# One written order for four engines in the turns of a packed attention and soft-MoE kernel

## The chip, the cores and the metric

The kernel runs on one core of a Trainium2 chip. The metric is the device time of one execution in microseconds. TensorE is PE in the tables (PEld its weight loads), VectorE DVE, ScalarE ACT, GpSimd POOL, and SyncE SP, which here only issues DMAs.

## What is computed

Shapes: q, k and v are 8 batches x 8 heads x 576 x 64, p holds 32 queries per head, phi is 512 x 32, w1 is 8 x 512 x 1024, w2 is 8 x 1024 x 512, and all is float32.

```python
def sm_attn(qq, kk, vv):
    a = softmax(scale * qq @ kk.T)
    return a @ vv
p_packed = sm_attn(p, k, v)
x = sm_attn(q, p_packed, p_packed)        # then [4608, 512]: heads side by side
logits = x @ phi
slot_input = softmax(logits, over rows).T @ x
slot_out[e] = relu(slot_input[e] @ w1[e]) @ w2[e]
out = softmax(logits, over slots) @ slot_out
```

Each softmax subtracts its maximum and adds 1e-9 to its sum.

## The kernel before

The work goes in 8 turns. Turn i has four heads (g = i % 2) of two batches (dd = i // 2, a "double"), so a pair of turns makes one double. In the loop over turns 0 to 6 (from L757), turn i has three kinds of work at once:

- For turn i + 1 the first scores. `kp` (L213) transposes k in 18 pieces on PE, into PSUM banks of four (t0 = 0, 4, 8), and copies each bank to kT; `s1` (L228) makes the 8 score products, the negated maximum nm on DVE (L250), the Exp on ACT (L254, its result a1) and a small copy a1e on POOL.
- For turn i the packed heads and the second scores. `ap` (L265) and `at` (L280) transpose a1 and copy it to a1T and a1tail; `ppm` (L288) multiplies with v into the bank m; `ppn` divides by the sums (rz), giving ppd; `pt` (L321) transposes ppd in the same bank and copies it to ppT in two halves; `mp` multiplies with phi. `qp` (L351) transposes q in 18 pieces and copies to qT. `s2p`, `s2m` and `s2s` (L370, L394, L400) make the second scores s in three parts c = 0, 1, 2, their maxima mx and the subtraction into a2, and `e2` (L431) is one Exp over all of a2.
- For turn i - 1 the rest. `n2` sums a2 on DVE (z, L442), takes the reciprocal (L449) and multiplies a2 on POOL (L450). `a2p` (L453) transposes a2 in 9 pieces and copies them to a2T, and `lg` (L470) makes the logits lp, which go to LT.

Every second turn (3 and 5) also finishes a double: `f1` to `f4`, `gz`, `gr`, `gt`, `gs` (L502 to L712) update the running maximum, the sums z_run and the slot inputs S_run (tiles post, mx, rw, gr, rt, rb). Each second turn prepares a new p (`pre_p`, L188, tile tp).

What sets the order: each helper issues its PE products and behind them their copies. `evac` (L81) gives a copy to ACT or DVE by a running count of estimated load, if no engine is named. In the loop no order is fixed; a scheduler arranges each engine's instructions by priority (the order of the code) and by when it thinks them ready. Turn 7 and what ends the attention stand in `manual_schedule` (L870), where the order of the code is the order on PE, DVE, ACT and POOL. Engines run their queues in order. PSUM banks rotate: `pstr` has 4, for k, q, a1, a2, tp, mx and the second scores, `ps1` holds one first score, `psm` one m, `psp` one of lp, post or gr.

DMAs are issued by SP in the order of the code: per turn v, k and q of later turns (L99 to L141), then the weights (L734, L741). q, k, v and the weights share a ring of 15 tiles of 1 MB (L57), so a load waits for the tile that stood there 15 loads earlier; their small tails share 6. Behind the loop more pools open for weights when others are closed. Behind the attention come layer 1 (hp, L991), layer 2 (so, L1040, and for the last expert sb, L1134), and the output.

Of the kernel before, what the change touches and what calls it, by code (L numbers as in the profile page):

```python
# [23 lines left out]
def pack_attention_soft_moe(  # L24
# [162 lines left out]

    def pre_p(dd):  # L188
        pn = pns[dd]
        pnd = kpool.tile([P, NG, 2, 2, D], F32, tag="pnd", name=f"pnd_{dd}")  # L190
        pT = kpool.tile([P, NG, 8, NS // 2, 2], F32, tag="pT", bufs=2, name=f"pT_{dd}")
        for x in range(2):
            nc.vector.tensor_copy(pnd[:, :, :, x, :], pn.rearrange("p g (s d) -> p g s d", s=2))
        tp = bank(pstr, f"tp{dd}")
        for g in range(NG):
            for j in range(2):
                nc.tensor.transpose(
                    tp[:, (2 * g + j) * P : (2 * g + j + 1) * P],
                    pnd[:, g, j].rearrange("p x d -> p (x d)"),
                    ident,  # L200
                )
        for g in range(NG):
# [118 lines left out]
    def pt(i):  # L321
# [3 lines left out]
        for b2 in range(2):  # L325
            nc.tensor.transpose(
                tp[:, b2 * P : (b2 + 1) * P], s["ppd"][:, b2].rearrange("p x d -> p (x d)"), ident
            )
        tpv = tp.rearrange("p (b h s) -> p b h s", b=2, h=4)
        nc.vector.tensor_copy(ppT[0:D, :, :, 1, :], tpv[0:D])  # L330
        nc.vector.tensor_copy(ppT[D:P, :, :, 0, :], tpv[D:P])  # L331

    def mp(i):
# [4 lines left out]
        for b2 in range(2):  # L338
            for a in range(2):
# [6 lines left out]
                )  # L346
        mm = lpool.tile([P, 2, NSLOT], F32, tag="mm", bufs=2, name=f"mm_{i}")
        nc.scalar.copy(mm.rearrange("p b x -> p (b x)"), mq)
        s["mm"] = mm

    def qp(i, m0, eng=None):  # L351
# [4 lines left out]
        if m0 == 0:  # L356
            s["qT"] = tpool.tile([P, 2 * T, P], F32, tag="qT", name=f"qT_{i}")
# [6 lines left out]
        evac(s["qT"][:, m0 : m0 + nt].rearrange("p t x -> p (t x)"), tp[:, 0 : nt * P], eng)  # L364
# [27 lines left out]

    def s2m(i, c):
# [6 lines left out]
    def s2s(i, c):  # L400
# [3 lines left out]
            s["a2"][:, t0 : t0 + nt].rearrange("p t h s -> p h t s"),  # L404
# [11 lines left out]
    def e2d(i, c):  # L416
# [3 lines left out]
            s["a2"][:, t0 : t0 + nt].rearrange("p t h s -> p h t s"),  # L420
# [33 lines left out]
    def a2p(i, c, eng=None):  # L454
# [15 lines left out]
    def lg(i, pool=psp):  # L470


        dd, g = divmod(i, NG)
        s = st[i]
        lp = bank(pool, f"lp_{i}")
        for b2 in range(2):
# [9 lines left out]
        for c in range(4):  # L486
# [6 lines left out]
            )  # L493
        if g == 0:
# [7 lines left out]
    def f1(dd):  # L502
        f1a(dd)
        f1b(dd)

    def f1a(dd):
# [8 lines left out]
        nc.scalar.activation(dL, LT, AF.Exp, bias=nm, scale=1.0, accum_out=zg)  # L515
        nc.vector.tensor_scalar_mul(mt, nm, -1.0)
        x["mt"], x["zg"], x["dL"] = mt, zg, dL

    def f1b(dd, pool=psp):
        x = du[dd]  # L520
        LT, dL = x["LT"], x["dL"]
        d = qpool.tile([P, T, NSLOT], F32, tag="d", name=f"d_{dd}")
        df = d.rearrange("p t s -> p (t s)")
        Ls = L_sb[:, dd].rearrange("p t s -> p (t s)")
        x["d"] = d

        b = bank(pool, f"post_{dd}")
        for y, src in enumerate((LT, dL)):
            for j in range(2):
                o = y * W + j * P  # L530
                nc.tensor.transpose(b[:, o : o + P], src[:, j * P : (j + 1) * P], ident)
        nc.vector.transpose(df[:, W : W + 32], dL[:, W : W + 32])
        nc.scalar.copy(df[:, 0:W], b[:, W : 2 * W])
        nc.vector.transpose(Ls[:, W : W + 32], LT[:, W : W + 32])
        nc.scalar.copy(Ls[:, 0:W], b[:, 0:W])
# [687 lines left out]
```

## Time and profile before

| | us |
|---|---|
| median of 3 runs | 222.86 |
| lowest and highest | 220.75, 227.43 |
| the profiled execution | 222.83 |
| its span in the trace | 221.1 |

The span goes from the first instruction to the last on the core; 1.7 us of the execution lie around it. Durations come from that one execution. In a timeline, instructions of one group that follow closely are merged: the start, then the stretch they take together, then their number, and in brackets how long the engine stood idle ahead of them and what released it. A product of float32 is two PE instructions in the trace for some shapes. [...]

### The profile page before, as it was taken

What the parts mean: (1) busy time and instruction counts of PE and PEld (TensorE: products, weight loads), DVE (VectorE), ACT (ScalarE), POOL (GpSimd) and SP (SyncE); (2) the same over time, 40 slices, a digit from 0 to 9 for tenths busy, and PEclk for the clock granted to TensorE, in tenths of its full rate; (3) what the DMA queues carried; (4) which work ended last, traced back from release to release, by engine and by line L of the source; (5) the groups of instructions that cost most, each with busy time, mean ns of one, the idle gap of its engine ahead of it and who ended that gap; (6) DMA issues with size and microseconds to landing.
All of it is one profiled execution on the core that took longest, in us unless ns stands there. A gap on an engine that the chain in (4) does not pass through costs nothing.

```text
span 221.1 us, 6708 instructions
## 1 busy us (share of the span) xinstructions
PE 188.4 (85%) x2811; PEld 127.8 (58%) x2811; DVE 120.5 (54%) x279; ACT 116.3 (53%) x253; POOL 25.0 (11%) x40
## 2 busy tenths in 40 slices
PE   1787799998996999899999988998999999989700
PEld 1655576685783688578688757875633333456300
DVE  2221576259387237648955717897679170288800
ACT  2277466956753675675675694745322000188800
POOL 3000003004003000400300220043021000000000
PEclk9999999999999799999999999999999999999955
DMA  4999999999999999579999989999789999159996
GB/s 134 325 312 318 334 342 334 289 267 337 306 314 298 360 313 355 145 246 390 412 406 406 387 299 385 345 397 411 261 314 350 414 406 407 59 209 414 408 416 262
DMA packets 39198, 72.33 MB, mean 327 GB/s; under 512 B 11648, under 2 KB 23168, under 8 KB 39168
## 3 DMA queue, kind: packets, MB, share of 16 engines
q1 hardware_dynamic: 39168, 71.90, 93.2%
q8 instruction: 22, 0.36, 0.7%
q14 instruction: 8, 0.07, 0.1%
HBM read 62.46 MB, written 9.44 MB: 325 GB/s over the span
## 4 chain that ended last, share of the span: by engine, by line
PE 53%; ACT 17%; DVE 10%; DMA 7%; issue 4%; SPq 3%; ACTq 0%; DVEq 0%
PE s L387 8%; PE kp L223 6%; PE s L243 6%; DMA v<-in_v_dram 6%; PE so L1040 5%; ACT a L254 5%; PE m L297 3%; PE op L1165 3%; ACT kT L88 3%; PE gr L641 3%; PE hp L991 2%; ACT qT L88 2%; PE ap L272 2%; PE lp L479 2%; ACT a1T L88 2%
## 5 line engine op out<-in xcount | busy, mean ns | idle before, releaser
L88 ACT COPY kT<-kp 128x512 f32<-128x512 f32 (+1 forms) x42 | 19.1, 484 | 24.9 <-PE kp L223 24.9
L450 POOL TENSOR_TENSOR a<-a,z 128x1152 f32<-128x1152 f32 (+1 forms) x8 | 16.0, 1996 | 71.2 <-DVE z L449 58.7
L223 PE MATMUL kp<-ident,k 128*128 128x128 f32 x128 | 20.9, 307 | 2.2 <-DMA k<-in_k_dram 1.3
L254 ACT ACTIVATE a<-s,nm 128x576 f32<-128x576 f32 x16 | 21.6, 1352 | 1.6 <-DVE nm L250 1.6
L88 ACT COPY qT<-qp 128x512 f32<-128x512 f32 (+1 forms) x40 | 20.2, 558 | 3.5 <-PE qp L363 3.1
L387 PE MATMUL s<-ppT,qT 128*64 128x64 f32 x576 | 20.6, 225 | 1.1 <-DVE ppT L331 0.3
L387 PEld LDWEIGHTS s<-ppT,qT 128*64 128x64 f32 x576 | 18.3, 138 | 4.8 <-ACT qT L88 3.7
L250 DVE TENSOR_REDUCE nm<-s 128x1 f32<-128x576 f32 x16 | 11.9, 745 | 16.8 <-PE s L243 16.8
L223 PEld LDWEIGHTS kp<-ident,k 128*128 128x128 f32 x128 | 16.1, 157 | 7.4 <-ACT a1T L88 1.7
L243 PE MATMUL s<-kT,pT 64*32 64x288 f32 x256 | 16.8, 437 | 3.8 <-ACT kT L88 3.0
L397 DVE TENSOR_REDUCE mx<-s 128x16 f32<-128x512 f32 (+1 forms) x24 | 12.5, 551 | 11.5 <-PE s L387 11.5
L363 PE MATMUL qp<-ident,q 128*128 128x128 f32 x128 | 18.2, 278 | 0.0
L88 ACT COPY a1T<-ap 128x512 f32<-128x512 f32 x16 | 8.7, 589 | 17.1 <-PE ap L272 17.1
L363 PEld LDWEIGHTS qp<-ident,q 128*128 128x128 f32 x128 | 15.1, 145 | 1.9 <-issue 1.9
L991 PE MATMUL hp<-w,xz 128*32 128x512 f32 x128 | 14.4, 594 | 0.5 <-DVE xz L1092 0.5
L442 DVE TENSOR_REDUCE z<-a 128x36 f32<-128x1152 f32 (+2 forms) x9 | 10.9, 1207 | 6.4 <-ACT a L433 6.4
L1165 PE MATMUL op<-sh,cT 128*128 128x512 f32 x35 | 12.7, 455 | 0.8 <-DVE cT L91 0.3
L1040 PE MATMUL so<-w,hT 128*32 128x512 f32 x112 | 12.4, 592 | 0.0
L91 DVE COPY ob<-op 128x512 f32<-128x512 f32 x17 | 11.3, 689 | 1.3 <-PE op L1165 0.9
L459 PE MATMUL a2p<-ident,a 128*128 128x128 f32 x72 | 11.0, 280 | 0.5 <-ACT a L419 0.4
L88 ACT COPY a2T<-a2p 128x512 f32<-128x512 f32 (+1 forms) x24 | 11.1, 510 | 0.6 <-PE a2p L459 0.5
L297 PE MATMUL m<-v,a1T 128*32 128x64 f32 x512 | 9.7, 221 | 1.9 <-ACT a1T L88 1.4
(156 smaller groups left out, 302.3 us busy)
## 6 DMA issues: line engine op xcount, KB each, us to landing
w<-in_moe_w_dram SPq DMA_DIRECT2D x64, 512.0 KB, 8.0
out_dram<-ob SPq DMA_DIRECT2D x11, 768.0 KB, 5.8
k<-in_k_dram SPq DMA_DIRECT2D x16, 512.0 KB, 6.6
q<-in_q_dram SPq DMA_DIRECT2D x16, 512.0 KB, 6.9
v<-in_v_dram SPq DMA_DIRECT2D x16, 512.0 KB, 7.4
kx<-in_k_dram SPq DMA_DIRECT2D x16, 64.0 KB, 6.1
qx<-in_q_dram SPq DMA_DIRECT2D x16, 64.0 KB, 6.5
vx<-in_v_dram SPq DMA_DIRECT2D x16, 64.0 KB, 6.9
```

The lines of the kernel that those rows point to most:

```text
L88: nc.scalar.copy(dst, src)
L223: nc.tensor.transpose(tp[:, j * P : (j + 1) * P], src, ident)
L243: nc.tensor.matmul(ps[hs, x, 0:HALF], pTs[dd][xs, g, 4 * b2 + h].rearrange("p a s -> p (a s)"), kT[xs, :, hs], start=True, stop=True,)
L254: nc.scalar.activation(a1.rearrange("p (r t x) -> p x t r", t=T, x=2), ps[:, :, 0:HALF].rearrange("p x (t r) -> p x t r", t=T), AF.Exp, bi ...
L297: nc.tensor.matmul(s["m"][hs, b2 * D : (b2 + 1) * D], s["a1T"][:, 4 * b2 + j, hs] if j < 4 else a1tail[:, b2, hs], vm[:, b2, h, j * D : (j ...
L363: nc.tensor.transpose(tp[:, j * P : (j + 1) * P], qf[:, o : o + P], ident)
L387: nc.tensor.matmul(o, s["qT"][:, m, 64 * x : 64 * x + 64], w, start=True, stop=True)
L397: nc.vector.tensor_reduce(mx, s[f"s2{c}"], axis=AX.X, op=ALU.max)
L450: eng.tensor_tensor(a2, a2, z2.unsqueeze(3).broadcast_to([P, nt, 4, NS]), op=ALU.mult)
L991: nc.tensor.matmul(hp[nh][32 * a : 32 * a + 32, :], xzf[:, (4 * e + a) * NSLOT : (4 * e + a + 1) * NSLOT], w1s[e, a // 2][:, a % 2, nh * 5 ...
L1040: nc.tensor.matmul(so[32 * a : 32 * a + 32, :], hTf[:, (NJ * e + j) * NSLOT : (NJ * e + j + 1) * NSLOT], w2s[e, j // 4][:, j % 4, :], star ...
L1165: nc.tensor.matmul(op, cT[:, o, :], sh, start=True, stop=True)
```

## The change

The helpers are cut into parts, so that a group of PE products and the copies of its result can stand apart, and every copy's engine is named. A function `parts(i)` gives the parts of turn i by name, and one string, `PAIR`, names some 135 parts of two turns (those of the second with a ') in the order in which they are issued, `:a` or `:d` behind a copy saying ACT or DVE. The loop goes over pairs, inside `manual_schedule` for PE, DVE, ACT and POOL. The last pair has only turn 6. `START` does the same for the first scores and q of turn 0. The finish of a double stays in its second turn, with `f1` now there too. The stretch behind the loop keeps its order with the new names. The products, the copies and the loads stay the same in number and kind; SP's order does not change.

```diff
-    def kp(i, b2):
-        kT = kpool.tile([P, T, P], F32, tag="kT", bufs=2, name=f"kT_{i}_{b2}")
-        for t0, nt in ((0, 4), (4, 4), (8, 1)):
-            tp = bank(pstr, f"kp_{i}_{b2}_{t0}")
...
-            evac(kT[:, t0 : t0 + nt].rearrange("p t x -> p (t x)"), tp[:, 0 : nt * P])
+    def kt(i, b2, t0):
+        tp = bank(pstr, f"kp_{i}_{b2}_{t0}")
+        for t in range(t0, min(t0 + 4, T)):
+            src = main[:, b2, t * P : (t + 1) * P] if t < 8 else tail[:, b2]
+            nc.tensor.transpose(tp[:, (t - t0) * P : (t - t0 + 1) * P], src, ident)
+    def ke(i, b2, t0, eng):
...
+        evac(
+            s[f"kT{b2}"][:, t0 : t0 + nt].rearrange("p t x -> p (t x)"),
+            s[f"kp{b2}{t0}"][:, 0 : nt * P],
+            eng,
+        )
...
+    PAIR = """
+        load ap0 ape0:d ap1 k04 ke04:a k00 ke00:a q0 ape1:d k08 m0 z2 ke08:a rz s10 q8 z2r qe0:a at n2
+        k10 q16 ate:a m1 mt0 qe16:a qe8:d s1m0 mt1 a22 q12 ke10:a a21 pre_c ppd a2e2:d s1x0 k14 qe12:d
...
+    with tc.manual_schedule(engines={EP.PE, EP.DVE, EP.Activation, EP.Pool}):
+        pre_p(0)
...
+        go(first, START)
+        for i in range(0, NSTEP, NG):
+            ops = {}
+            for y in range(NG):
+                if i + y < NSTEP - 1:
+                    ops.update((x + "'" * y, f) for x, f in parts(i + y).items())
+            for x in PAIR:
+                if x == "load":
+                    loads(i)
+                elif x == "load'":
+                    loads(i + 1)
+                else:
+                    go(ops, [x])
```

The names in PAIR: k04 is a group of transposes of k (b2 = 0, t0 = 4) and ke04 its copy, q8 and qe8 the same of q, ap and ape of a1, a2 and a2e of a2; m and mt are the products with v and with its tail; s10, s1m0, s1x0 and s1c0 the first scores, their maximum, Exp and the copy on POOL; s20, s2m0 and s2s0 the second scores, maximum and subtraction of part 0.

Three places show what the order on an engine becomes. First PE at the head of turn 2, before. The scores s_3_0 belong to turn 3, kp to its k, and the last numbers tell buffers apart.

```order
L272 MATMUL ap_0_756<-ident,a_2_0_584 128x128 x4
L272 MATMUL ap_1_762<-ident,a_2_1_630 128x128 x4
L223 MATMUL kp_0_0_769<-ident,k_476 128x128 x4
L223 MATMUL kp_0_4_775<-ident,k_476 128x128 x4
L223 MATMUL kp_0_8_781<-ident,kx_477 128x128
L297 MATMUL m_784<-v_470,a1T_755 32x64 x32
L283 MATMUL at_817<-ident,a1e_573 128x128
L223 MATMUL kp_1_0_855<-ident,k_476 128x128 x2
L243 MATMUL s_3_0_841<-kT_0_768,pT_431 32x288
L297 MATMUL m_784<-vx_471,a1tail 32x64 x8
L243 MATMUL s_3_0_841<-kT_0_768,pT_431 32x288 x7
L223 MATMUL kp_1_0_855<-ident,k_476 128x128 x2
```

And PE there in the changed kernel:

```order
L303 MATMUL ap_0_757<-ident,a_2_0_618 128x128 x4
L303 MATMUL ap_1_764<-ident,a_2_1_711 128x128 x4
L235 MATMUL kp_0_4_769<-ident,k_647 128x128 x4
L235 MATMUL kp_0_0_776<-ident,k_647 128x128 x4
L410 MATMUL qp_0_782<-ident,q_653 128x128 x4
L235 MATMUL kp_0_8_788<-ident,kx_648 128x128
L337 MATMUL m_790<-v_641,a1T_762 32x64 x16
L259 MATMUL s_3_0_812<-kT_0_774,pT_507 32x288 x8
L410 MATMUL qp_8_821<-ident,q_653 128x128 x4
L319 MATMUL at_830<-ident,a1e_733 128x128
L235 MATMUL kp_1_0_833<-ident,k_647 128x128 x4
L410 MATMUL qp_16_838<-ident,qx_654 128x128 x2
```

Between the transposes of k and the first scores stand a group of q and half of m; m's second half and its tail follow, with the rest of k, later.

Second, ACT in the same place before: a2T and LT end turn 1's work, kT_0 is for turn 3, e2 is the row with 128x1152.

```order
L497 COPY LT_703<-lp_694 128x288
L88 COPY a1T_755<-ap_0_756 128x512
L88 COPY a1T_755<-ap_1_762 128x512
L88 COPY kT_0_768<-kp_0_0_769 128x512
L433 ACTIVATE a_1_673<-a_1_673 128x1152
L88 COPY kT_0_768<-kp_0_4_775 128x512
L88 COPY kT_0_768<-kp_0_8_781 128x128
L286 COPY a1tail<-at_817 64x128 x2
L88 COPY kT_1_854<-kp_1_0_855 128x512
L88 COPY kT_1_854<-kp_1_4_861 128x512
```

And in the changed kernel:

```order
L491 ACTIVATE a_1_713<-a_1_713 128x1152
L579 COPY LT_731<-lp_721 128x288
L88 COPY kT_0_774<-kp_0_4_769 128x512
L88 COPY kT_0_774<-kp_0_0_776 128x512
L88 COPY kT_0_774<-kp_0_8_788 128x128
L88 COPY qT_828<-qp_0_782 128x512
L88 COPY a1tail<-at_830 64x128 x2
L88 COPY qT_828<-qp_16_838 128x256
L88 COPY kT_1_878<-kp_1_0_833 128x512
L282 ACTIVATE a_3_0_893,rz_892<-s_3_0_812,nm_865 128x2x9x32
```

The two copies a1T have gone to DVE, e2 and LT stand ahead of all kT copies, and copies of qT stand between the two kT.

Third, DVE in the finish of turn 3 before: z sums a2 (its last step is the reciprocal that POOL's product waits for), mr, m and m_run are the running maximum, rw the weighted sum.

```order
L545 TENSOR_REDUCE mr_1061<-mx_1059 1x32
L550 COPY m_0_1062<-mr_1061 1x128
L442 TENSOR_REDUCE z_2_0_1131<-a_2_940 128x36
L532 STREAM_TRANSPOSE d_1018<-dL_1014 128x32
L558 COPY m_run<-m_0_1062 1x32
L91 COPY kT_0_1066<-kp_0_8_1079 128x128
L448 TENSOR_SCALAR z_2_0_1131<-z_2_0_1131 128x36
L449 RECIPROCAL z_2_0_1131<-z_2_0_1131 128x36
L586 TENSOR_SCALAR rw_1139<-rep,w_1136,zg_1013 128x32
L313 TENSOR_TENSOR ppd_1129<-m_1082,rz_839 128x256
```

And in the changed kernel:

```order
L500 TENSOR_REDUCE z_2_0_1118<-a_2_973 128x36
L505 TENSOR_SCALAR z_2_0_1118<-z_2_0_1118 128x36
L506 RECIPROCAL z_2_0_1118<-z_2_0_1118 128x36
L661 TENSOR_REDUCE mr_1135<-mx_1115 1x32
L666 COPY m_0_1136<-mr_1135 1x128
L674 COPY m_run<-m_0_1136 1x32
L628 STREAM_TRANSPOSE L_sb<-LT_731 128x32
L356 TENSOR_TENSOR ppd_1158<-m_1025,rz_892 128x256
L714 TENSOR_SCALAR rw_1177<-rep,w_1162,zg_1071 128x32
```

The sum and reciprocal now stand ahead of the maximum's three steps, and those ahead of rw; ppd moved ahead of rw.

## Rows read from the trace of the kernel before

**Rows 1.** Windows: wall, busy time of PE, PEld, DVE, ACT, POOL, PEclk, DMA.

```profile
16.20:29.78 13.58, 11.07 (x227) 8.11 (x225) 5.88 (x14) 8.64 (x19) 0.71 (x3) 1.00 1.05 331
29.78:45.87 16.09, 15.09 (x269) 11.20 (x265) 8.45 (x20) 11.38 (x25) 2.61 (x3) 1.00 1.03 304
45.87:62.67 16.80, 15.42 (x270) 11.62 (x271) 10.40 (x22) 10.96 (x24) 2.61 (x3) 1.00 1.03 321
62.67:84.55 21.88, 19.77 (x342) 14.79 (x340) 11.90 (x30) 13.08 (x30) 2.60 (x3) 0.92 1.09 321
84.55:101.04 16.49, 15.49 (x274) 11.74 (x271) 10.03 (x23) 10.58 (x23) 2.61 (x3) 1.00 0.79 252
101.04:119.55 18.51, 18.11 (x344) 13.91 (x342) 12.65 (x34) 12.83 (x30) 2.61 (x3) 1.00 1.02 403
119.55:135.17 15.62, 14.62 (x266) 11.04 (x265) 8.42 (x17) 10.58 (x23) 2.60 (x3) 1.00 0.94 353
135.17:160.70 25.53, 22.61 (x401) 17.17 (x397) 19.98 (x61) 13.88 (x36) 4.24 (x3) 1.00 0.95 360
```

**Rows 2.** Timeline of PE in turn 4, its last row from turn 5.

```profile
87.10 1.10 PE L297 MATMUL m<-v,a1T 128*32 128x64 f32 x64
...
93.34 0.72 PE L243 MATMUL s<-kT,pT 64*32 64x288 f32 x16 [0.60 <-ACT kT L88]
...
94.16 0.60 PE L459 MATMUL a2p<-ident,a 128*128 128x128 f32 x4
94.59 0.60 PE L363 MATMUL qp<-ident,q 128*128 128x128 f32 x4
...
97.16 1.15 PE L387 MATMUL s<-ppT,qT 128*64 128x64 f32 x32
...
99.45 1.39 PE L387 MATMUL s<-ppT,qT 128*64 128x64 f32 x40
...
117.59 0.64 PE L479 MATMUL lp<-a2T,mm 128*32 128x256 f32 x8
```

**Rows 3.** Chain of work that ended last, in turn 5: start, us, what.

```profile
108.91 1.85 PE gr L641 x48
```

**Rows 4.** Timeline of turn 3: PE, DVE and POOL.

```profile
70.46 0.41 PE L589 MATMUL mx<-rw,ones 128*128 128x32 f32 x2 [1.55 <-DVE rw L586]
...
68.51 1.89 DVE L586 TENSOR_SCALAR rw<-rep,w,zg 128x32 f32<-128x32 f32 x1 [0.42 <-ACT w L577]
...
68.24 2.13 POOL L450 TENSOR_TENSOR a<-a,z 128x1152 f32<-128x1152 f32 x1 [9.63 <-ACT a1tail L286]
```

**Rows 5.** Groups by shape, DVE and ACT: count, busy us, mean ns, idle before.

```profile
L397 DVE TENSOR_REDUCE mx<-s 128x16 f32<-128x512 f32 x16 | 11.0, 686 | 11.5 <-PE s L387 11.5
L397 DVE TENSOR_REDUCE mx<-s 128x4 f32<-128x128 f32 x8 | 2.2, 279 | 0.0
L91 DVE COPY kT<-kp 128x512 f32<-128x512 f32 x4 | 2.7, 686 | 3.1 <-PE kp L223 3.1
...
L88 ACT COPY kT<-kp 128x512 f32<-128x512 f32 x28 | 15.8, 588 | 23.5 <-PE kp L223 23.5
L433 ACT ACTIVATE a<-a 128x1152 f32<-128x1152 f32 x7 | 8.2, 1172 | 0.0
```

**Rows 6.** DMA share and rate by window (last columns); then the weights' instructions.

```profile
5.00:85.00 80.00, 71.04 (x1172) 52.71 (x1171) 39.46 (x88) 49.17 (x108) 8.78 (x13) 0.98 1.05 320
85.00:188.60 103.60, 98.13 (x1535) 63.63 (x1537) 64.82 (x161) 51.29 (x117) 14.19 (x14) 1.00 0.94 354
170.00:175.00 5.00, 5.00 (x54) 2.19 (x58) 1.90 (x6) 1.07 (x2) 0.00 (x0) 1.00 1.02 410
...
L741 SPq DMA_DIRECT2D w<-in_moe_w_dram x32: 328/376/1350, 130.2 to 180.6; - x32
L1134 PE MATMUL sb<-w,hT x32: 379/379/403, 188.7 to 191.4; 128*32 128x256 f32 x32
DMA to landing us min/median/max: 3.2/8.0/11.7
```

More of the change, by code (lines that the diff above doesn't have):

```diff
@@ L300, in ppm, with ppr @@
                     vm[:, b2, h, j * D : (j + 1) * D] if j < 4 else vt[:, h, :],
-                    start=(b2 == 0 and j == 0),
-                    stop=(b2 == 1 and j == 4),
-                )
+                    start=(s["mn"] == 1),
+                    stop=(s["mn"] == 10),
+                )
+    def ppr(i):
+        rz = st[i]["rz"]
+        nc.vector.tensor_scalar_add(rz, rz, EPS)
+        nc.vector.reciprocal(rz, rz)
     def ppn(i):
@@ L514, in f1a, with f1x, f1l, f1t @@
         nc.vector.tensor_reduce(nm, LT, axis=AX.X, op=ALU.max, negate=True)
-        nc.scalar.activation(dL, LT, AF.Exp, bias=nm, scale=1.0, accum_out=zg)
         nc.vector.tensor_scalar_mul(mt, nm, -1.0)
-        x["mt"], x["zg"], x["dL"] = mt, zg, dL
+        x["nm"], x["mt"], x["zg"], x["dL"] = nm, mt, zg, dL
+    def f1x(dd):
+        x = du[dd]
+        nc.scalar.activation(x["dL"], x["LT"], AF.Exp, bias=x["nm"], scale=1.0, accum_out=x["zg"])
     def f1b(dd, pool=psp):
-        x = du[dd]
-        LT, dL = x["LT"], x["dL"]
+        f1l(dd, pool)
+        f1t(dd)
+        f1c(dd)
+        f1d(dd)
+        f1e(dd)
+        f1f(dd)
+    def f1l(dd, pool=psp, y=0):
+        x = du[dd]
+        src = x["LT" if y == 0 else "dL"]
+        if "post" not in x:
+            x["post"] = bank(pool, f"post_{dd}")
+        for j in range(2):
+            o = y * W + j * P
+            nc.tensor.transpose(x["post"][:, o : o + P], src[:, j * P : (j + 1) * P], ident)
+    def f1t(dd, pool=psp):
+        f1l(dd, pool, 1)
+    def f1c(dd):
+        x = du[dd]
+        Ls = L_sb[:, dd].rearrange("p t s -> p (t s)")
+        nc.vector.transpose(Ls[:, W : W + 32], x["LT"][:, W : W + 32])
+    def f1d(dd):
+        x = du[dd]
         d = qpool.tile([P, T, NSLOT], F32, tag="d", name=f"d_{dd}")
+        x["d"] = d
         df = d.rearrange("p t s -> p (t s)")
[L524 to L535, printed above, removed]
+        nc.vector.transpose(df[:, W : W + 32], x["dL"][:, W : W + 32])
+    def f1e(dd):
+        x = du[dd]
+        nc.scalar.copy(x["d"].rearrange("p t s -> p (t s)")[:, 0:W], x["post"][:, W : 2 * W])
+    def f1f(dd):
+        x = du[dd]
+        nc.scalar.copy(L_sb[:, dd].rearrange("p t s -> p (t s)")[:, 0:W], x["post"][:, 0:W])
     def f2(dd):
+        f2t(dd)
+        f2m(dd)
+    def f2t(dd):
         x = du[dd]
@@ L542, in f2, with f2m @@
         nc.tensor.transpose(bm[0:1, 0:P], x["mt"], ident)
+    def f2m(dd):
+        x = du[dd]
+        bm = x["bm"]
         mr = small.tile([1, NSLOT], F32, tag="mr", bufs=1, name=f"mr_{dd}")
@@ L561, in f3, with f3p @@
     def f3(dd):
+        f3p(dd)
+        f3x(dd)
+    def f3p(dd):
         x = du[dd]
@@ L588, in f4, with f4p @@
         )
+        x["rw"] = rw
+    def f4p(dd):
+        x = du[dd]
         nc.tensor.matmul(
-            x["bm"][:, W + NSLOT : W + 2 * NSLOT], ones, rw, start=True, stop=True
+            x["bm"][:, W + NSLOT : W + 2 * NSLOT], ones, x["rw"], start=True, stop=True
         )
@@ L679, in gbg @@
         )
-    def gt(dd):
-        for g in range(NG):
-            gtg(dd, g)
-        for g in range(NG):
-            gbg(dd, g)
     def gsg(dd, g):
@@ new lines, in pack_attention_soft_moe @@
+    """.split()
+    START = """
+        k04 k00 k18 ke04:a ke00:a k08 k10 ke08:a s10 ke10:a k14 ke18:d ke14:a q4 s1m0 s1x0 s1c0 qe4:a
+        s11 q8 s1m1 s1x1 q0 qe0:a q16 q12 qe8:d qe12:a s1c1 qe16:a
+    """.split()
+    with tc.manual_schedule(engines={EP.PE, EP.DVE, EP.Activation, EP.Pool}):
+        pre_p(0)
+        first = parts(-1)
+        first.update((f"q{m0}", (qt, 0, m0)) for m0 in range(0, 2 * T, 4))
+        first.update((f"qe{m0}", (qe, 0, m0)) for m0 in range(0, 2 * T, 4))
+        go(first, START)
[11 more added lines that the diff above has]
+                    go(ops, [x])
+        pes.close()
+        extras = [extra(0)]
```

342 lines of the change are left out of this document (196 added, 146 removed).

## Prediction

> **What bounds the kernel now.** I read the trace in three steps: first a table of the seven turns and of the stretch behind them, then one turn's PE instructions, then what DMA does. In [rows 1] each line is one turn, cut where its first transpose of a1 (the first Exp's output) starts, and the last line is the stretch from turn 7 to the first weight product. The seven turns take 118.97 us of the span of 221.1, 13.58 to 21.88 us each. PE's busy time is near the wall in every one, but the end of each product is modelled and overlaps the next, so busy is not work. Work is read from starts: in [rows 2] four transposes start 0.43 us before the next four, 0.1075 each. A plain turn (1 or 6) then has 56 transposes (18 of k, 18 of q, 9 of a2, 8 of a1, one of its tail, 2 of ppd) at 0.1075 = 6.0; 80 instructions of m at 1.10/64 = 1.4; two score groups at 0.72 = 1.4; the second scores 1.15 + 1.39 = 2.5; lp 0.6; mp 0.3 by estimate from its eight pieces. That is 12.2 us. Turns 2 and 4 have four more transposes (12.6). Turns 3 and 5 carry a double turn's finish: gr 1.85 [rows 3], and for post, mx, gt and gs some 1.6 by estimate from their number, so 15.7. Turn 0 has no q, a2 and lp: 8.7 + 0.4 = 9.1. The sum is 90.1.
>
> So PE stands still, or stretched, for 118.97 - 90.1 = 28.9 us: 4.5, 3.9, 4.2, 6.2, 3.9, 2.8 and 3.4 by turn. Those 28.9 us are what a change of order can work on. No other engine is full: in turns 3 and 4 together (38.4 us) DVE is busy 21.9 and ACT 23.7 [rows 1]. The loop is bound by PE waiting in its queue for copies, which wait in theirs. [...]
>
> **What is removed.** No product and no copied byte goes. The order changes on four engines and some copies change engine. Per pair, DVE gets nine copies of 512 columns where it had one, at 0.69 us, and gives one of each turn's two ppT copies to ACT; ACT loses eight at 0.59 [rows 5]. For turns 3 and 4, DVE goes from 21.9 by 8 x 0.69 less some 0.4 of small ones to about 27 us, ACT from 23.7 to about 20. PE's stream for the same pair is 28.3. So DVE and PE are both near full, and a pair of 32 us has 4 us to lose on PE, 5 on DVE.
>
> **What PE still waits for.** I walk the written order with these durations.
>
> First turn of a pair. The first scores of the next step need three copies of kT on ACT. These stand behind e2 and LT of the turn before, and e2 behind the four DVE steps of the last second-score groups. From the end of the product s_0: DVE's two maxima 0.69 + 0.28 and two subtractions of the same shapes, 1.9, e2 1.17, LT 0.4 by estimate (288 columns, where 512 take 0.59), kT 0.59 + 0.59 and 0.3 by estimate: together 4.9 [rows 5]. PE has meanwhile s_2 0.2, lp 0.6, eight transposes of a1, nine of k, four of q (21 x 0.1075 = 2.3) and half of m, 0.6: 3.7. Wait 1.2. Before, these kT copies ran around e2 too, but PE had little besides m to put in front of the scores. Later in this turn the a1 transposes follow nm and Exp, and four PSUM banks rotate through ap, k, q and a2 groups, each reused when a copy on one of two engines is done: 1.3 us by estimate, some six hand-offs of 0.2. Sum 2.5.
>
> Second turn. The k08 group takes the bank of s_0, which is free when its subtraction on DVE is done. Behind s_0 stand on DVE mx, a1T and the subtraction, 0.69 each, and mm, LT and two steps on rz, 1.0 by estimate: 3.1. PE has tp, ap, k04, lp and 32 products of m, 12 x 0.1075 + 0.6 + 1.1 = 3.0, and 0.3 of latency: wait 0.4. The rest is bank hand-offs, 1.7 by estimate. Sum 2.1.
>
> A second turn with a finish has one more. The normalisation of a2 on POOL takes 2.13 us, and rw on DVE, 32 columns wide, took 1.89 us in just that window: it started 0.27 behind POOL and ended with it [rows 4]. In the new order the reciprocal that starts POOL stands right ahead of the copies of the running maximum (f2m), which read SBUF, and PE's f3p waits for them. Of 2.13 us the products of m's tail and half of gr ahead of f3p cover 0.4 + 0.9; 0.8 stay, and 0.6 for gr's bank, which must wait for the copy of L on ACT. Sum 3.5.
>
> [...]
>
> **Sum.** Turn 0 is a chain of latencies whatever the order, 3.9 us; turn 6 has no partner to fill it, 2.8. So 3.9 + 2.1 + 2.5 + 3.5 + 2.5 + 3.5 + 2.8 = 20.8 us against 28.9, and the loop ends 8.1 us earlier. The bounds: the hand-offs that I estimate are 1.3 or 1.7 in each of turns 1 to 6, some 9 us in all; if they were nothing, 17 us would go, and if they were twice as long, the loop would end 1 us later than now. I take 8.1, since they stand for copies of 0.59 and 0.69 us that are mostly done when PE comes to their bank. The start (0 to 16.2 us) follows landing loads; a few copies there change engine, which I cost at nothing, 0.6 either way (one copy).
>
> **What DMA does with it.** The stretch behind the loop is the same code, 25.53 us [rows 1]. The last weights are issued at 180.6 and land a median 8.0 later, 188.6; the first product of the last layer starts at 188.7 [rows 6]. Both must come earlier. From 5 to 85 us DMA is full (share 1.05, 320 GB/s with q, k and v). From 85 to 188.6 its share is 0.94, which leaves 6.2 us of the 103.6; by rate, 354 GB/s there against 410 in a full stretch, it is 36.7 MB that could take 89.4 us, 14.2 less [rows 6]. The gaps are SP's waits for tiles that an earlier loop frees earlier. Between 6.2 and 14.2 I take the middle, 10, which is over 8.1; for the share of cases in which it is under I charge 0.5.
>
> The profiled execution took 222.83 us with a span of 221.1, and the median of three is 222.86, so the sum is made against 222.8: 222.8 - 8.1 + 0.5 = 215.2.
>
> **Rivals.** A: DMA holds the end. For it: the share says that only 6.2 us are free, and some of the gaps come from pools that open late in the stretch behind the loop, whose order stays. Against it: the rate says 14.2. If half of the 6.2 is got back, the end is 222.8 - 3.1 = 219.7, whatever the loop wins. Chance 0.13.
>
> B, slower: DVE becomes the bound. The place is the head of each turn: both a1T copies stand on DVE behind the subtractions, and m, z and nm behind them. If each of the eight copies that moved per pair made PE late by its own 0.69 us, that is 5.5 us a pair and 19 in three and a half, against the 8.1 that I win without it: 11 us longer, 234; with half of them late it is 1.5 longer, 224.3. It decides when more than some 3.4 of the eight are late. I put it at six, 229. For it: both queues run strictly in the written order, and POOL can hold DVE for 2.13 us in every turn. Against it: DVE was idle for 16.5 us of turns 3 and 4, and still is for 5 in a pair of 32. Chance 0.09.
>
> C: the waits only move. PE loses the 1.55 us at rw and the clock's fall, gains as much at banks; 2 us are left, 221. For it: turn 5 already waits just 2.8 us with the old order. Against it: six other turns wait 3.4 to 6.2. Chance 0.10.
>
> D: new stalls of PE pull the granted clock down again. In turn 3 it fell around one wait of 1.55 us; the walk has one of 1.2 in each pair. Turn 3 waits 2.3 us more than turn 1 (6.2 against 3.9), so three such pairs cost 7 us: 222. Chance 0.05. The forecast keeps 0.63.
>
> **Numbers.** Forecast 215.2. The ends: with no hand-offs the loop wins 17 us and DMA allows 14.2, 208.6, so the range begins at 208.5; upward it takes in A, C and D to 223. About 0.09 lies above it with B, 0.08 below. Faster by over 2% (below 218.4; 2% is about what a measurement tells from no change): the forecast and a tail of A, 0.70. Within 2%: A, C, D and the weak end of the forecast, 0.20. Slower by over 2%: B, 0.10.
>
> **What would show it.** Right: a table by turn with turn 3 near 19 us and turns 1, 2, 4 near 14 to 15; the stretch behind still 25.5; the last layer's products starting near 181; a DMA share of 0.97 or more behind 85 us. Of the steps: PE waiting about 1 us for kT at the first scores of each even turn; a DVE step of 1.5 to 2 us inside POOL's 2.13. Wrong: turns over 16 us with DVE busy over 14; a granted clock below 1 in several turns; or a loop 8 us shorter with products of the last layers waiting for weights (A).

## The result and the profile after

The changed kernel takes 212.43 us (median of 4, 211.34 to 213.37), the kernel before on the same chip 223.12 (220.75 to 227.43): ratio 0.9553, 95% interval [0.9459, 0.9647]. The run of 227.43 was a slow one and is left out of the ratio. The time lies in the range, 2.8 us under the forecast of 215.2. The profiled execution took 212.3 us, its span is 210.5.

Windows of the changed kernel, in the columns of [rows 1], of which the last three are the granted TensorE clock as a share of its full speed (PEclk), the mean busy share of the 16 DMA engines, and GB/s: the pairs of turns 0-1, 2-3 and 4-5, turn 6, the stretch behind the loop, layers 1 and 2 up to the last expert; then four windows that answer to [rows 6].

```profile
17.96:43.09 25.13, 22.88 (x491) 18.41 (x490) 17.42 (x37) 17.21 (x37) 3.27 (x6) 1.00 1.07 323
43.09:75.46 32.37, 30.70 (x619) 24.51 (x610) 27.13 (x61) 20.30 (x44) 5.22 (x7) 1.00 1.07 328
75.46:108.27 32.81, 31.14 (x622) 24.97 (x612) 27.88 (x64) 20.50 (x45) 5.21 (x7) 1.00 1.06 360
108.27:121.68 13.41, 12.67 (x273) 10.62 (x264) 11.19 (x26) 9.02 (x18) 2.65 (x4) 1.00 1.02 405
121.68:147.50 25.82, 22.66 (x407) 17.23 (x398) 19.94 (x60) 13.86 (x36) 4.24 (x3) 1.00 1.03 406
147.50:178.81 31.31, 30.74 (x264) 10.52 (x268) 14.16 (x30) 3.41 (x5) 2.12 (x2) 1.00 0.95 380
...
5.00:85.00 80.00, 71.87 (x1320) 56.72 (x1320) 55.80 (x124) 49.19 (x103) 11.14 (x15) 1.00 1.06 323
85.00:150.00 65.00, 60.07 (x1145) 46.04 (x1145) 53.54 (x130) 36.60 (x85) 9.69 (x10) 1.00 1.04 394
150.00:165.00 15.00, 14.43 (x114) 4.59 (x114) 7.16 (x17) 2.82 (x4) 2.12 (x2) 1.00 1.02 408
165.00:172.00 7.00, 7.00 (x76) 2.67 (x72) 3.75 (x10) 0.59 (x1) 0.00 (x0) 1.00 1.02 406
```

Against [rows 1] the pairs take 25.13, 32.37 and 32.81 us where they took 29.67, 38.68 and 35.00, turn 6 takes 13.41 for 15.62: 103.72 for 118.97, 15.25 less. The loop starts 1.76 later (17.96 for 16.20), so it ends 13.5 earlier. The stretch behind it is 0.3 longer. From the first product of layer 1 to the first of the last expert it is 31.3 us where it was 27.9 (160.76 to 188.65), so 3.4 go back; the end is 0.7 shorter. Together -13.5 + 0.3 + 3.4 - 0.7 = -10.5, and the span fell by 10.6. The two ends of that stretch in the kernel before:

```profile
160.76 8.81 PE L991 MATMUL hp<-w,xz 128*32 128x512 f32 x80 [0.46 <-DVE xz L1092]
...
188.65 1.07 PE L1134 MATMUL sb<-w,hT 128*32 128x256 f32 x16
```

DMA is full from 5 to 172 us (share 1.02 to 1.06), at 394 to 408 GB/s behind 85 us where it had 354 [rows 6]. What that does shows in the timeline of PE's weight loads in layer 1, and of PE beside it:

```profile
149.98 0.24 PEld L1143 LDWEIGHTS hp<-w,xz 128*32 128x32 f32 x4 [0.19 <-DMA w<-in_moe_w_dram]
151.25 0.17 PEld L1143 LDWEIGHTS hp<-w,xz 128*32 128x32 f32 x8 [1.03 <-DMA w<-in_moe_w_dram]
155.09 0.14 PEld L1143 LDWEIGHTS hp<-w,xz 128*32 128x32 f32 x2 [1.12 <-DMA w<-in_moe_w_dram]
156.37 0.17 PEld L1143 LDWEIGHTS hp<-w,xz 128*32 128x32 f32 x8 [1.14 <-DMA w<-in_moe_w_dram]
...
147.50 7.37 PE L1143 MATMUL hp<-w,xz 128*32 128x512 f32 x48 [0.46 <-DVE xz L1244]
155.09 1.04 PE L1143 MATMUL hp<-w,xz 128*32 128x512 f32 x2 [0.21 <-DMA w<-in_moe_w_dram]
156.37 3.66 PE L1143 MATMUL hp<-w,xz 128*32 128x512 f32 x30 [0.23 <-DMA w<-in_moe_w_dram]
```

The first 80 hp products took 8.7 us before the change (from 160.76 to the cT transposes at 169.50) and take 12.5 now; the four waits of the weight loads for DMA add up to 3.48. The chain that ended last runs through four loads of weights in a row, from turn 6 into layer 1 (start, us):

```profile
115.14 9.43 DMA w<-in_moe_w_dram
124.58 11.21 DMA w<-in_moe_w_dram
135.81 10.28 DMA w<-in_moe_w_dram
146.10 10.22 DMA w<-in_moe_w_dram
```

So from 115 to 156 us it is the weights that set the end, and PE's work in turn 6 and behind the loop has some room.

### The profile page after: what moved, and what is told of

Its sections match the earlier page's. It is cut to its first block, busy times and chain, and to the rows that moved or that the text cites. A ratio compares the mean times of both kernels' runs of the same rounds, so it can differ in the third digit from the quotient of the medians.

```text
span 210.5 us, 6703 instructions
## 1 busy us (share of the span) xinstructions
PE 179.2 (85%) x2811; PEld 123.8 (59%) x2811; DVE 137.1 (65%) x311; ACT 105.1 (50%) x221; POOL 25.0 (12%) x40
## 4 chain that ended last, share of the span: by engine, by line
PE 39%; DMA 23%; DVE 18%; ACT 8%; issue 2%; POOL 2%; SPq 1%; POOLq 0%; DVEq 0%; ACTq 0%
DMA w<-in_moe_w_dram 20%; PE so L1192 6%; PE hp L1143 4%; PE kp L235 4%; PE op L1317 3%; PE s L443 3%; PE s L259 3%; PE qp L410 3%; ACT a L491 3%; DMA kx<-in_k_dram 3%; DVE a L466 3%; DVE z L500 2%; POOL a L515 2%; DVE mx L460 2%; PE ap L303 2%
## 5 line engine op out<-in xcount | busy, mean ns | idle before, releaser
L88 ACT COPY kT<-kp 128x512 f32<-128x512 f32 (+1 forms) x40 | 19.7, 532 | 16.2 <-PE kp L235 16.1
L235 PE MATMUL kp<-ident,k 128*128 128x128 f32 x128 | 20.4, 294 | 0.5 <-DVE a L466 0.2
L410 PE MATMUL qp<-ident,q 128*128 128x128 f32 x128 | 19.4, 278 | 0.0
L1143 PE MATMUL hp<-w,xz 128*32 128x512 f32 x128 | 17.5, 596 | 1.0 <-DVE xz L1244 0.5
L235 PEld LDWEIGHTS kp<-ident,k 128*128 128x128 f32 x128 | 15.6, 151 | 3.1 <-issue 0.9
L88 ACT COPY qT<-qp 128x512 f32<-128x512 f32 (+1 forms) x27 | 13.9, 531 | 2.1 <-PE qp L410 1.6
L259 PE MATMUL s<-kT,pT 64*32 64x288 f32 x256 | 12.0, 432 | 3.1 <-ACT kT L88 1.8
L460 DVE TENSOR_REDUCE mx<-s 128x16 f32<-128x512 f32 (+1 forms) x24 | 12.5, 547 | 1.5 <-PE s L443 1.5
L337 PE MATMUL m<-v,a1T 128*32 128x64 f32 x512 | 10.5, 222 | 1.7 <-issue 1.5
L491 ACT ACTIVATE a<-a 128x1152 f32<-128x1152 f32 x7 | 8.2, 1168 | 7.5 <-DVE a L466 7.5
L296 POOL COPY a1e<-a 128x64 f32<-128x64 f32 x16 | 3.8, 238 | 66.9 <-ACT a L282 64.3
```

The source lines that it names most:

```text
L88: nc.scalar.copy(dst, src)
L235: nc.tensor.transpose(tp[:, (t - t0) * P : (t - t0 + 1) * P], src, ident)
L259: nc.tensor.matmul(ps[hs, x, 0:HALF], pTs[dd][xs, g, 4 * b2 + h].rearrange("p a s -> p (a s)"), kT[xs, :, hs], start=True, stop=True,)
L410: nc.tensor.transpose(tp[:, j * P : (j + 1) * P], qf[:, o : o + P], ident)
L460: nc.vector.tensor_reduce(mx, s[f"s2{c}"], axis=AX.X, op=ALU.max)
L1143: nc.tensor.matmul(hp[nh][32 * a : 32 * a + 32, :], xzf[:, (4 * e + a) * NSLOT : (4 * e + a + 1) * NSLOT], w1s[e, a // 2][:, a % 2, nh * 5 ...
```

## The experiments

The theory: the written order puts other products in front of those that wait, which shortens the loop; the weights, with DMA full, then hold layer 1. Rivals: the engines that are named do it; leaving the scheduler does it; the 3.4 us are not DMA's.

**Engines.** Every `:d` of PAIR becomes `:a`, and of pte both halves go to DVE. (In the lines shown of PAIR the line breaks are set alike on both sides; the first line stands for the rest.)

```diff
-        load ap0 ape0:d ap1 k04 ke04:a k00 ke00:a q0 ape1:d k08 m0 z2 ke08:a rz s10 q8 z2r qe0:a at n2
+        load ap0 ape0:a ap1 k04 ke04:a k00 ke00:a q0 ape1:a k08 m0 z2 ke08:a rz s10 q8 z2r qe0:a at n2
```

> The changed kernel's written order kept on all engines; only the engine of a copy changes: every copy named for DVE goes to ACT, the ppT copies alone stand on DVE, nearly as the kernel before had them. Theory (the order, what stands in front of a waiting product, gives the gain): most of the gain stays. ACT takes nine copies of 512 columns more in a pair, 9 x 0.59 = 5.3 us, so 20.3 goes to about 26 of the 32.4 us of pair 2-3, and some waits come back, about 1 us a pair: 215 to 217 us. Rival (the balance of the two copying engines gives the gain): the loop falls back to about 119 us and the time to 220 to 224.

218.12 us, ratio 0.9818 [0.9757, 0.9879] to the kernel before, run beside it. Pair 2-3 by windows, and PE's view of waits in the loop:

```profile
46.22:80.74 34.52, 30.89 (x618) 24.50 (x609) 21.73 (x50) 24.57 (x55) 5.21 (x7) 1.00 1.06 326
...
PE qp L410 <- ACT a1T L88: 3.1, 3, 1.1
PE ap L303 <- ACT qT L88: 2.0, 3, 0.8
```

ACT has 24.6 us for 20.3, and PE now waits at a1T and qT copies. Layer 1 starts at 156.13, 8.6 us behind the changed kernel, and the time is only 5.7 longer: a miss by a microsecond, between theory and rival. The loop takes 113.13 us (17.75 to 130.88): with nearly all copies on ACT the new order takes 5.8 us off the 118.97 of the kernel before, with DVE's share 15.25. So with this order the named engines are worth 9.4 us of loop.

**Order, fixed.** The string rewritten in the old order of the code, for instance

```diff
-        load ap0 ape0:d ap1 k04 ke04:a k00 ke00:a q0 ape1:d k08 m0 z2 ke08:a rz s10 q8 z2r qe0:a at n2
+        load ap0 ape0:d ap1 ape1:d k00 ke00:a k04 ke04:a k08 ke08:a m0 m1 at ate:a mt0 mt1 rz ppd z2
+        z2r n2 s10 s1m0 s1x0 s1c0 k10 ke10:a k14 ke14:a k18 ke18:d pt pte0:a pte1:d q0 qe0:a
```

> The changed kernel's copies, engines and fixed order as a mechanism, but the string holds the parts in the order in which the code of the kernel before issued them, each copy right behind its product. Theory (the order): worse than both, since neither a scheduler nor the string brings other products forward; each of the some 14 groups of transposes of a turn waits for its bank or copy, 2 to 4 us a turn more than before: 235 to 250 us. Rival (leaving the scheduler, with engines named, gives the gain): about 212 to 216.

255.72 us (251.83 to 260.51), above the theory's range; the lowest is still 29 us above the kernel before. Its loop takes 149.8 us (18.36 to 168.18) at a mean granted clock of 0.89, and even if PE was held for all that the clock lacked, 16.5 us, this order, fixed, costs 14 more than the 118.97 of the kernel before. Fixing an order is no gain in itself.

**Priority only.** `manual_schedule` around the loop goes; the string stays as the order of the code.

> The changed kernel's parts and engines, its string being only the priority: the loop is given to the scheduler, as the loop of the kernel before was, and not fixed. Theory (the order that is fixed): the scheduler moves many instructions by when it thinks them ready, so a good part of the gain goes: 216 to 224. Rival (the parts, and the engines that are named, give the gain, however arranged): 211 to 214.

212.72 us, ratio 0.955 [0.9509, 0.9591], as with the fixed order: here the theory failed. The scheduler kept nearly all of the written order on PE (43 rows of difference in some 400, where the kernel before has over 240). Layer 1 starts at 149.62 in the profiled execution, 2.1 us later than with the fixed order; half of that is left at the last expert (179.88 for 178.81), and the medians differ by 0.3. That leaves order against engines, so the same with the old order of the code as priority:

> The changed kernel's parts and engines under the scheduler, and the string in the code order of the kernel before (the string of e2_codeorder, without the fixed order): beside e2_sched only the written order differs, beside the kernel before only the cut into parts and the engines. Theory (the written order counts, as priority or fixed): layer 1 starts 8 to 13 us later than in e2_sched (149.6), at 158 to 162, and the time is 219 to 225. Rival (the cut and the named engines give the gain): layer 1 starts before 152, time 211 to 214.

224.54 us, ratio 1.0072 [1.0038, 1.0106]. The loop by windows with the new order as priority, then with the old one:

```profile
17.59:123.17 105.58, 98.01 (x1975) 78.86 (x1974) 83.00 (x186) 67.15 (x142) 16.33 (x21) 1.00 1.06 345
```

```profile
16.89:137.81 120.92, 110.25 (x1974) 83.46 (x1973) 84.16 (x185) 65.69 (x142) 16.33 (x21) 0.97 0.99 321
```

and the old order's layer 1:

```profile
163.26 8.82 PE L1144 MATMUL hp<-w,xz 128*32 128x512 f32 x80 [0.46 <-DVE xz L1245]
```

Same engines, same scheduler, old order: layer 1 starts 13.6 us later than with the new order as priority, and 2.5 later than in the kernel before. The loop alone is 15.3 us longer; its granted clock stood at 0.50 from 27.7 to 31.1 and from 109.6 to 113.0, which can account for at most 3.4 of them, so 11.9 stay with the order. The order is the cause. The engines add to it, as the run with the copies on ACT showed; under the old order they bring nothing.

**One filler.** The group q0 and half of m moved from ahead of the first scores to behind them.

```diff
-        load ap0 ape0:d ap1 k04 ke04:a k00 ke00:a q0 ape1:d k08 m0 z2 ke08:a rz s10 q8 z2r qe0:a at n2
+        load ap0 ape0:d ap1 k04 ke04:a k00 ke00:a ape1:d k08 z2 ke08:a rz s10 q0 m0 q8 z2r qe0:a at n2
```

> In the even turns of the changed kernel the group q0 and the first half of m no longer stand in front of the first scores s10 on PE but right behind them; nothing else moves. Theory (they cover the wait for kT): the wait at the first scores grows from 0.5 by up to 0.43 + 0.28 (four transposes, 16 products), to about 1.2 us, in turns 2, 4 and 6 (in turn 0, which has no q, by 0.28); that is 1.2 to 2.4 us by the start of layer 1, and 0.3 to 1.5 in the time, since the weights' loads hide a part. Rival (the place of single groups does not matter, PE has slack behind): layer 1 starts within 0.6 us of the changed kernel's.

PE at the first scores of turn 2, in the changed kernel:

```profile
46.87 0.72 PE L259 MATMUL s<-kT,pT 64*32 64x288 f32 x16 [0.52 <-ACT kT L88]
```

and in this one, with the first products of layer 1:

```profile
47.22 0.72 PE L259 MATMUL s<-kT,pT 64*32 64x288 f32 x16 [1.56 <-ACT kT L88]
...
152.28 9.78 PE L1144 MATMUL hp<-w,xz 128*32 128x512 f32 x80 [0.46 <-DVE xz L1245]
```

The wait grew by 1.04, more than the 0.7 expected, and turn 7 starts at 124.82 where it was 121.86 in the repeat of the changed kernel beside it, three such turns. Layer 1 starts 5.0 us later in this execution: some 2 us more came behind the loop, where the granted clock from 140 to 152.28 was 0.80. Its first 80 hp products wait for no weights, and at the last expert 1.8 of the 5.0 are left (181.15 for 179.39 in the repeat); this execution took 214.63 at a mean granted clock of 0.967. The other four had 0.979 to 0.985, as the changed kernel has, and took 212.51 to 212.70, so the median is 212.58, ratio 0.9558 [0.9512, 0.9604], and the repeat's 212.71, 0.9562 [0.9521, 0.9603]: the 3 us of loop are not seen at the end. The repeat:

> The changed kernel itself, once more, so that the next runs stand beside it on the same chip: 212 to 213 us, layer 1's first product at 147.5, within 1 us.

**Half of w2.** In `load_w`:

```diff
+        if lay == 2 and c == 1:
+            w2s[e, c] = w2s[e, 0]
+            return
```

> The changed kernel without the second half of every expert's w2 load (8 MB of 16 less in w2: the first half is used twice, so eight tiles of 1 MB and 16 DMAs go). Theory (behind the loop the DMA queue, full to 172 us, holds layer 1 and gives back 3.4 us of the loop's gain): the stretch from the first product of layer 1 to the first of the last expert falls from 31.3 to about 28 us, as before the change, and the time by 3 to 3.6 us, to about 209. Rival (the 3.4 us are PE's or the hidden copies' own): that stretch stays at 31 and the time within 0.8 us of 212.4.

209.06 us, ratio 0.937 [0.9314, 0.9426], 3.4 us less. The timeline:

```profile
146.87 8.81 PE L1146 MATMUL hp<-w,xz 128*32 128x512 f32 x80 [0.45 <-DVE xz L1247]
...
174.77 1.07 PE L1289 MATMUL sb<-w,hT 128*32 128x256 f32 x16
```

80 products in 8.81 with no wait, as before the change; 27.9 us to the last expert. The same edit on the kernel before:

> The kernel before, with the edit of e3_after_half: the second half of every expert's w2 isn't loaded (the first half is used twice). Theory (DMA held nothing in the kernel before, only in the changed one): ratio to the kernel before 0.995 to 1.0, the stretch from layer 1's first product to the last expert's stays at 27.9 us. Rival (less DMA traffic makes everything faster, whatever it waits for, so e3_after_half tells nothing of the change): about 0.985, as there.

225.2 us, ratio 1.0124 [1.0072, 1.0176]: no gain, but slower, which neither side expected. Layer 1 starts at 162.92, 2.2 us later than before, and the stretch to the last expert is 29.0 us, not 27.9. The windows of before and of this run around layer 1's start:

```profile
160.00:165.00 5.00, 4.54 (x48) 1.63 (x50) 3.32 (x4) 1.16 (x1) 0.48 (x1) 1.00 0.88 312
```

```profile
160.00:165.00 5.00, 4.54 (x36) 2.66 (x36) 3.30 (x6) 0.37 (x1) 0.00 (x0) 0.50 0.99 374
```

The granted clock stood at 0.50 in that stretch and fell in a part of the one before (150 to 160: 0.91). The last gr and gs products, from the second group of 24 to layer 1, then take 1.2 us more (4.52 for 3.35) and the first 80 hp products 1.1 (9.89 for 8.81). Those 2.3 us, 0.7 that turn 7 starts later and 0.3 that PE stands longer in front of its products m (0.76 for 0.49) are the 3.3 us by which this execution is longer, so no gain hides behind the clock: DMA held nothing in the kernel before.

**POOL's hold and the start.**

```diff
-        ke18:a f1t' k10' q8' f1d' f2t' f1e' z2' q0' z2r' mt1' mt0' f2m' f1c' qe8':a gr1' ppd' f1f'
+        ke18:a f1t' k10' q8' f1d' f2t' f1e' z2' q0' mt1' mt0' f2m' z2r' f1c' qe8':a gr1' ppd' f1f'
...
-        k04 k00 k18 ke04:a ke00:a k08 k10 ke08:a s10 ke10:a k14 ke18:d ke14:a q4 s1m0 s1x0 s1c0 qe4:a
+        k04 k00 ke04:a ke00:a k08 ke08:a k18 k10 s10 ke10:a k14 ke18:d ke14:a q4 s1m0 s1x0 s1c0 qe4:a
```

> The changed kernel with two local edits. In the finish (turns 3 and 5) the steps of the running maximum stand in front of the reciprocal that starts POOL's product, not behind it; at the start the group k18, whose tail of k lands late, stands behind k08. Theory (POOL's product holds the DVE copies of the maximum, and the start lost 1.76 us by the order): the copy m takes 0.1 to 0.3 us where it took 2.18, PE's wait of 0.72 for it goes in both turns, and turn 0 starts at 16.2 to 17.0 where it was 17.96; layer 1 starts 2 to 3 us earlier, and the time falls by no more than 1 us, since the weights hold what comes behind. Rival (POOL's hold only moves to the next DVE step, and the start waits for its loads anyway): layer 1 starts within 0.7 us of the changed kernel's.

212.32 us, ratio 0.9555 [0.9501, 0.9609]. Turn 3's timeline, in the changed kernel (DVE, POOL, PE):

```profile
63.96 2.18 DVE L666 COPY m<-mr 1x128 f32<-1x128 f32 x1
...
63.94 2.13 POOL L515 TENSOR_TENSOR a<-a,z 128x1152 f32<-128x1152 f32 x1 [7.38 <-DVE mr L661]
...
66.20 0.38 PE L686 MATMUL mx<-ones,m 1*128 1x1 f32 x2 [0.72 <-DVE m L666]
```

and with the steps exchanged:

```profile
64.48 0.21 DVE L666 COPY m<-mr 1x128 f32<-1x128 f32 x1
...
66.70 1.00 DVE L714 TENSOR_SCALAR rw<-rep,w,zg 128x32 f32<-128x32 f32 x1 [0.94 <-ACT w L702]
...
65.54 2.13 POOL L515 TENSOR_TENSOR a<-a,z 128x1152 f32<-128x1152 f32 x1 [8.40 <-ACT kT L88]
...
65.99 0.38 PE L686 MATMUL mx<-ones,m 1*128 1x1 f32 x2
```

The copy of 128 numbers takes 0.21 for 2.18; the hold moves in part to rw (1.00 for 0.30, ending 0.03 behind POOL's product), where products cover it. In turn 5 PE's wait was 0.79 and is gone too. The pairs with a finish take 0.8 and 0.9 us less (43.67 to 75.25, to 107.19). The start came out the other way: the wait for k's tail fell from 1.86 to 1.11, but turn 0 started at 19.45, not 17.96 (the last section has the reason). So layer 1 starts 1.5 earlier, at 146.01, less than the 2 to 3 expected, and PE gives back more than that there: 34.5 us to the last expert, for 31.3.

**Layer 1 in the order in which weights land.**

```diff
...
-        layer1a(0, range(QE))
+        for a, e in ((0, 0), (0, 2), (0, 1), (QE, QE), (QE, QE + 1), (0, 3)):
+            layer1a(a, [e])
...
         hidden(0)
-        layer1a(QE, [QE])
         for u in range(2):
             cp(0, u)
-        layer1a(QE, [QE + 1])
-        layer1b(0)
         layer1a(QE, [QE + 2])
+        layer1b(0)
```

> The changed kernel, and in layer 1 the products of experts 4 and 5 in front of those of expert 3, whose two weight tiles land last of the first group (PE waited for them at 155.09 and 156.37); expert 2 in front of 1; the products of expert 6 behind the first cT group. Nothing is left out. Theory (the weights' landing order holds PE in layer 1): the stretch from the first product of layer 1 to the first of the last expert falls from 31.3 to 28 or 29 us and the time by 2 to 3.3 us, to about 209.5 to 210.5. Rival (DMA's end holds the last layers whatever PE does before): the wait moves to w2's last tiles, time within 0.8 us of the changed kernel's.

211.28 us, ratio 0.9484 [0.9415, 0.9552], and once more:

> The kernel of e7_layer1_order once more, beside e10_all on the same chip: ratio to the kernel before 0.945 to 0.952, time 210.5 to 211.8.

210.38 us, 0.9461 [0.9417, 0.9506]. The timeline of the first run (209.36 us, the lowest of its four):

```profile
146.11 11.23 PE L1143 MATMUL hp<-w,xz 128*32 128x512 f32 x96 [0.46 <-DVE xz L1244]
...
174.91 0.60 PE L1285 MATMUL sb<-w,hT 128*32 128x256 f32 x4
175.83 1.06 PE L1285 MATMUL sb<-w,hT 128*32 128x256 f32 x12 [0.31 <-DMA w<-in_moe_w_dram]
```

The stretch falls to 28.8, as expected, and to 29.4 when run again; of the 2 to 3.3 us in the time 1.4 and 2.3 came (against the repeat's 212.71). The wait is now on w2's last tile, as the rival said, but the time did fall by more than its 0.8. It is the fastest version that leaves nothing out. With the two edits before it:

> The edits of e9_f2m_start and of e7_layer1_order together. Theory (DMA bounds the kernel now: its loads end near 175 us whatever PE does): layer 1 starts 2 to 3 us earlier than in e7, PE then waits 2 to 3 us more for weights of layers 1 and 2, and the time is within 0.8 us of e7's, 210 to 211.5. Rival (the loop still sets the end): 208 to 209.5.

211.05 us, 0.9493 [0.9446, 0.9539], within 0.8 of the run beside it. But the condition of the theory did not come about: layer 1 starts at 146.93, where it starts at 146.73 in the run beside it. The loop is 2.0 us shorter (101.86 for 103.89), and the start, with turn 0 at 19.66 for 17.44, loses 2.2. So this run doesn't show what an earlier layer 1 would be worth.

## Why the prediction was right, and where its sizes were off

**What bounds it, and the removed waits: right.** The loop was bound by PE waiting in its queue, no product went, and the order alone moves layer 1 by 13.6 us and the loop by 15.3 at equal engines, at most 3.4 of it by the clock. DVE's and ACT's loads in turns 3 and 4 were forecast at 27 and 20 us; pair 2-3 shows 27.1 and 20.3.

**The sum of the waits: too large.** By the step's own count of work (90.1 us), 103.72 - 90.1 = 13.6 us of waits are left, not 20.8: 3.8 in the first pair (forecast 6.0), 4.1 and 4.5 in the next (6.0 each), 1.2 in turn 6 (2.8). The wait for kT was 0.5, not 1.2, and the estimates of the bank hand-offs, which the prediction set at "1.3 or 1.7 in each of turns 1 to 6", can't hold: with the other terms kept, some 4 us of their 9 are left. The 0.3 us of latency in the wait for the bank of s_0 no run shows: what stands in the traces is 0.04 us from the end of a copy of kT (93.30, turn 4 before) to the scores that wait for it, and 0.06 from the end of the copy m (66.14, turn 3 after) to its product. In the timeline of turn 1 before, the waiting that the order takes out looks like this:

```profile
34.36 0.67 PE L243 MATMUL s<-kT,pT 64*32 64x288 f32 x2
34.96 0.43 PE L297 MATMUL m<-vx,a1tail 128*32 128x64 f32 x16
35.32 0.71 PE L243 MATMUL s<-kT,pT 64*32 64x288 f32 x14
```

Two score products take 0.60 us to the next start, fourteen take 0.64, and no wait is named: it hides in the modelled end. PE's idle in the loop (wall less busy) fell only from 9.4 to 6.3 us; the other 12 us of the gain sat inside "busy".

**The start: cost at nothing, 0.6 either way; it cost 1.76.** PE's products up to turn 0 are the same in number; its waits among them grew. Before, then after:

```profile
9.09 1.94 PE L223 MATMUL kp<-ident,k 128*128 128x128 f32 x8 [1.03 <-DMA k<-in_k_dram]
15.27 0.72 PE L243 MATMUL s<-kT,pT 64*32 64x288 f32 x16 [0.61 <-ACT a L254]
```

```profile
9.64 0.69 PE L235 MATMUL kp<-ident,kx 128*128 128x128 f32 x2 [1.86 <-DMA kx<-in_k_dram]
15.72 0.72 PE L259 MATMUL s<-kT,pT 64*32 64x288 f32 x16 [1.37 <-ACT a L282]
```

k18 in front of k08 made PE wait 0.8 us more for a load (k's tail). As much comes from the second group of the first scores (s11): before, 16 transposes of q stood ahead of it, in START only four, and the wait for the Exp in front of it grew by 0.8; the other 14 pieces of q came behind and held up turn 0. The run that moved k18 changed the first part alone.

**POOL's hold: right.** 0.8 was charged at f3p; 0.72 was measured in turn 3 and 0.79 in turn 5, and the edit above gives it back. In turn 3 the copy m began 0.02 us behind POOL's product of 2.13 and ended 0.07 behind it; of its 2.18 us PE, which had products in front of f3p, waited for 0.72. B counted on such a hold in every turn. In the kernel before, a DVE step was long beside that product in three (the two copies pnd 1.51 in turn 2, for 0.48 in turn 4, where they stand ahead of it; rw 1.89 in turn 3; z_run 1.80 in turn 5, for 0.19 in turn 5 of the changed kernel); nm took 0.76 beside it in turns 1 and 2 and the copies of ppT 0.42 to 0.43 in turns 1, 4 and 6, as they do elsewhere.

**DMA: the step that failed.** "For the share of cases in which it is under I charge 0.5": 3.4 were given back. The limit was sized fairly (between 6.2 and 14.2, taken as 10; the last weight is issued 11.5 us earlier, at 169.1), but it was laid against a win of 8.1, and the loop won 13.5. The place was wrong too: the walk looked at the last weights and the last layer, and PE waited for weights among the first 80 products of layer 1, which take the weights in another order than they land. Two errors of opposite sign, 5.4 us too little won in the loop and 2.9 too little charged in layer 1, with 0.4 gained in the stretches behind, leave the 2.9 us by which the profiled 212.3 is under the forecast. That they cancelled in part is luck. Rival A named the limit that came, DMA, with the wrong time, 219.7. B did not come: DVE was busy 27.1 of 32.4 us and PE waited less. C fell with the loop, and D with turn 3's clock of 1.00 and rw's 0.30 us; before, the clock of turn 3 stood at 0.50 from 71.2 to 74.6, from 0.7 us behind the end of the wait at rw, and that the wait pulled it down was not shown.

## What to carry to other kernels

Where engines run their queues in order, write down which products stand between a producer's copy and its consumer; it was worth 12 to 15 us of loop here, together with DVE's share of the copies, and a scheduler given that order as priority kept it. When one stage shortens, size the next limit against the largest win that the bounds allow, not against the likeliest. And once DMA is full, a loop that was 3 us longer, or a layer 1 that started 1.5 us earlier, made no difference at the end that could be measured (8.6 us later cost 5.7); consuming weights in the order in which they land gained 1.4 to 2.3 us.

## What was not expected of the hardware

The clock: behind the loop, the kernel before and its run with half of w2 have the same products in the same order, with the same named waits of 0.65 and 0.46 us ahead of layer 1, and only in the second it fell, to 0.50. In the run with one filler moved it fell to 0.80 over 12 us, with DMA full (share 1.01), and in the one with the new order as priority to 0.51 from 145.1 to 152 (24 gr products 1.66 us there, for 0.99). What sets it off stays open. At the start eight transposes of q took 1.09 us from 16.37 in the changed kernel and 1.97 from 16.41 with k18 moved, with 1.00 in the row of the granted clock for both:

```profile
16.41 1.97 PE L410 MATMUL qp<-ident,q 128*128 128x128 f32 x8
```

Here the products show what that row doesn't. In the trace of the changed kernel the record of the granted clock begins at 13.9 us; ahead of it the row's 1.00 stands for no record, and the products run at about half the later rate: 16 first scores take 1.21 us at 11.54 and 0.72 at 15.72, eight transposes of k 1.97 at 5.80 and 1.04 at 19.74. With k18 moved the low rate lasts longer: the second 16 first scores take 1.21 at 15.27 and four transposes of q 1.06 at 18.60, for 0.60 at 17.52, and only then come eight of k in 1.04, at 20.45. The other run with k18 moved shows the same (1.21 at 15.59), while in each of the ten profiled executions that keep START as it was the second 16 first scores, which start between 14.80 and 16.77, take 0.72. It is where the start's edit lost its gain, 1.9 us from the start of the second group of first scores to turn 0; why the full rate came later there is not shown.
